# Convolution and low-rank mixer on one core: PSUM as one ring of four buffers, second product lagging by half a group, convolution a round earlier

## The chip, the cores and the metric

The kernel runs on one core of a Trainium2 chip. The metric is the device time of the kernel in microseconds. Before the change it is 365.75 us, the median of three runs (364.59, 365.75, 366.5). A trace of one further execution shows when each engine worked: TensorE (PE, with its weight loads as PEld), VectorE (DVE), ScalarE (ACT), GpSimd (POOL) and SyncE (SP, which only issues DMAs here).

## The reference

The input x has 8 batches of 4224 rows and 192 columns. It goes through a causal depthwise convolution of 7 taps, with softmaxed weights shared by the 24 columns of each of 8 heads, and then through a mixer: a low-rank product along the rows (rank 32), an add, and a two-layer product along the columns with a relu between.

```
w = softmax(weight)                       # 8 heads x 7 taps
y[b,s,h,:] = sum_k w[h,k] * xpad[b,s+k,h,:]
h = (y^T @ U @ V)^T                       # U: 4224 x 32, V: 32 x 4224
u = y + h
out = u + relu(u @ w_ch1) @ w_ch2         # 192 -> 768 -> 192
```

## The kernel before

The rows of all batches are cut into 264 tiles of 128 rows, 33 per batch, and 8 tiles make a group: 33 groups. The instructions of each engine run in the order in which the program writes them (manual_schedule), and a loop of 34 rounds (L596 to L613) writes that order out. Round g does the following:

- `mix_quad(g + 2)` (L414), twice, ahead of the chunks and behind them: four matmuls for the low-rank product of four tiles (L426), and two VectorE adds of y into u (L438, or three with L446 where a batch ends between two tiles).
- `h1_chunk(g, m)` for m = 0 to 5 (L486): six matmuls for the first product (L495), in three pairs that each work on the two halves of 64 rows at once, then a relu into rl_sb, on ScalarE for chunks 0, 2, 4 and 5 (L505) and on VectorE for chunks 1 and 3 (L507).
- `w2_step(g - 1, n)` for n = 0 to 47, six in each of eight pieces (L509): the second product of the group one round back. Six matmuls make one tile (L516). After every second tile VectorE adds u and writes o_sb (L525), and SP stores it (L532).
- between the pieces, steps for other batches, sorted by piece: `turn_by_dma(g + 2)` after piece 2 (a transposing DMA on SP, L477), and, for the next batch nb, the convolution and the low-rank product.

A convolution unit `conv_two` (L326) makes two heads of 21 or 12 tiles with two matmuls of 504 or 288 columns (L336) and one eviction to y (ScalarE L346; VectorE L348 only for batches 0 and 1). A batch has eight units. Rows at the start of each tile, which need the tile before, come from `conv_halo` (L352): eight matmuls (L359), two ScalarE copies (L368) and a store on SP to a scratch in memory (L376). `put_halo` (L379) writes them over y with a DMA on SP (L380), after all units. `low_rank` (L385, matmuls L393) then reduces y over the batch, and `fold` (L405) finishes it. With last = 33*nb//8 - 3, that is 1, 5, 9, 13, 17, 21 and 25 for batches 1 to 7, the units of batch nb run in rounds last-4 to last-1, two in each, put_halo after piece 5 of round last-1, low_rank after piece 3 and fold after piece 5 of round last. Batch 1 has all units in round 0; batch 0 is made before the loop.

x is loaded by POOL's queue (L85) into two buffers, so the load of batch nb+2 waits for the convolution of batch nb; the rows for the halo go through a scratch in memory, with a load on POOL (L94) and a second on SP (L99). These loads are written at the end of round last of batch nb. y has three buffers, u five, uT four, rl_sb two, o_sb six.

PSUM has eight banks. Six are three buffers of two banks each (`big`, L71), used by everything but the second product, taken in turn. The other two are two buffers of one bank (`chps`, L514), each for two tiles of the second product. An allocation waits until the engines are done with the one whose buffer it takes.

Of the kernel before, what the change touches and what calls it, by code (L numbers as in the profile page):

```python
# [11 lines left out]
F32 = mybir.dt.float32  # L12
# [3 lines left out]
def kernel(  # L16
# [11 lines left out]
    P = nc.NUM_PARTITIONS  # L28

    B, S, D = x.shape  # L30
# [5 lines left out]
    HB = P // 2  # L36
# [6 lines left out]
    NG = NTOT // GT  # L43
# [21 lines left out]
    rls = ctx.enter_context(tc.tile_pool(name="rls", bufs=2))  # L65
    outs = ctx.enter_context(tc.tile_pool(name="outs", bufs=6))

    big_ps = ctx.enter_context(tc.tile_pool(name="big_ps", bufs=3, space=bass.MemoryType.PSUM))
    w2_ps = ctx.enter_context(tc.tile_pool(name="w2_ps", bufs=2, space=bass.MemoryType.PSUM))

    def big(dtype=F32):  # L71
        return big_ps.tile([P, 2, BK * 4 // mybir.dt.size(dtype)], dtype, name="big")
# [8 lines left out]
    def new_x(b):  # L81
        x_tiles[b] = xs.tile([P, NT + 1, D], BF16, name="x_sb")

    def load_x(b, s0, s1):
        nc.gpsimd.dma_start(  # L85
            out=x_tiles[b][:, 1 + s0 : 1 + s1, :],
            in_=x[b, s0 * P : s1 * P, :].rearrange("(j p) d -> p j d", p=P),
        )

    def load_halo(b):  # L90

        hx_dr = dram.tile([HP, NT - 1, D], BF16, name="hx_dr")
        src = x[b, P - HALO : P - HALO + HP, :]
        nc.gpsimd.dma_start(  # L94
            out=hx_dr[:],
            in_=bass.AP(src.tensor, src.offset, [[D, HP], [P * D, NT - 1], [1, D]]),
        )
        hx = hxs.tile([HJ * HP, HS, D], BF16, name="hx_sb")
        nc.sync.dma_start(out=hx[:], in_=hx_dr[:].rearrange("p (j s) d -> (p j) s d", s=HS))  # L99
        hx_tiles[b] = hx  # L100
# [122 lines left out]
    for c in range(KC):  # L223
# [10 lines left out]
        in0=cps[:, 0, 0 : KC * H]  # L234
# [9 lines left out]
    for q in range(P // Q):  # L244
        rows = slice(q * Q, (q + 1) * Q)
        n = SP if q < P // Q - 1 else Q
# [79 lines left out]
    def conv_two(b, s0, s1, hh, on_act, bands):  # L326

        if b not in y_tiles:
            y_tiles[b] = ys.tile([P, NT, D], BF16, name="y_sb")
        x_sb, y_sb = x_tiles[b], y_tiles[b]  # L330
        n = (s1 - s0) * GS
        cps = big()
        for q in range(2):
            hc = slice((hh + q) * GS, (hh + q + 1) * GS)
            for w in range(bands):
                nc.tensor.matmul(  # L336
                    out=cps[:, q, 0:n],
                    lhsT=band_sb[:, hh + q, w, :],
                    rhs=x_sb[:, 1 + s0 - w : 1 + s1 - w, hc],
                    start=(w == 0),  # L340
                    stop=(w == bands - 1),
                )
        src = cps[:, :, 0:n].rearrange("p q (j c) -> p q j c", c=GS)
        dst = y_sb[:, s0:s1, hh * GS : (hh + 2) * GS].rearrange("p j (q c) -> p q j c", q=2)
        if on_act:
            nc.scalar.activation(out=dst, in_=src, func=ACT.Copy)  # L346
        else:
            nc.vector.tensor_copy(out=dst, in_=src)  # L348
# [3 lines left out]
    def conv_halo(b):  # L352

        hx = hx_tiles[b]
        n = HALO * HJ
        hps = big()
        H2 = H // 2
        for hh in range(H):
            nc.tensor.matmul(  # L359
                out=hps[:, hh // H2, (hh % H2) * HS * GS : (hh % H2 + 1) * HS * GS],  # L360
                lhsT=halo_band[:, hh, :],
                rhs=hx[:, :, hh * GS : (hh + 1) * GS],
                start=True,
                stop=True,
            )
        hy = hys.tile([n, HS, D], BF16, name="hy_sb")
        for h in range(2):
            nc.scalar.activation(  # L368
                out=hy[:, :, h * H2 * GS : (h + 1) * H2 * GS].rearrange(
                    "p s (h c) -> p h s c", c=GS  # L370
                ),
                in_=hps[0:n, h, 0 : H2 * HS * GS].rearrange("p (h s c) -> p h s c", s=HS, c=GS),
                func=ACT.Copy,
            )
        hy_dr = dram.tile([n, HS, D], BF16, name="hy_dr")
        nc.sync.dma_start(out=hy_dr[:], in_=hy[:])  # L376
        hy_tiles[b] = hy_dr

    def put_halo(b):  # L379
        nc.sync.dma_start(  # L380
            out=y_tiles[b][0:HALO, 1:NT, :],
            in_=hy_tiles[b][:].rearrange("(c j) s d -> c (j s) d", j=HJ),
        )

    def low_rank(b, j0, j1):  # L385
        y_sb = y_tiles[b]
        n = P // R
        if b not in tps_tiles:
            tps_tiles[b] = big()
        tps = tps_tiles[b]  # L390
        for j in range(j0, j1):
            q = j % n
            nc.tensor.matmul(  # L393
                out=tps[q * R : (q + 1) * R, 0, 0:D],
                lhsT=U_by_tile[:, :, j],
                rhs=y_sb[:, j, :],
                start=(j < n),
                stop=(j >= NT - n),
            )
        if j1 == NT:  # L400
            tf = tfs.tile([P, D], F32, name="tf_sb")
            nc.vector.tensor_copy(out=tf[:], in_=tps[:, 0, 0:D])  # L402
            tt_tiles[b] = tf
# [80 lines left out]
    rl_tiles, ch_tiles = {}, {}  # L484
# [24 lines left out]
    def w2_step(g, n):  # L509

        t, m = divmod(n, MC)
        i = t // 2
        if t % 2 == 0 and m == 0:
            ch_tiles[g, i] = w2_ps.tile([P, 2, D], F32, name="chps")  # L514
        chps = ch_tiles[g, i]
        nc.tensor.matmul(  # L516
            out=chps[:, t % 2, :],
            lhsT=rl_tiles[g][:, m, t, :],
            rhs=W2_sb[:, m, :],
            start=(m == 0),  # L520
            stop=(m == MC - 1),
        )
        if t % 2 == 1 and m == MC - 1:
            o_sb = outs.tile([P, 2, D], F32, name="o_sb")
            nc.vector.tensor_tensor(  # L525
                out=o_sb[:].rearrange("p t (k r) -> p t k r", r=HB),
                in0=chps[:].rearrange("p t (k r) -> p t k r", r=HB),
                in1=u_tiles[g][:, i].rearrange("p k t r -> p t k r"),
                op=ALU.add,
            )  # L530
            r0 = (g * GT + 2 * i) * P
            nc.sync.dma_start(  # L532
                out=out_rows[r0 : r0 + 2 * P, :].rearrange("(s p) d -> p s d", p=P),
                in_=o_sb[:],
            )
# [3 lines left out]
    i = 0  # L539
# [15 lines left out]
    load_halo(2)  # L555


    W2N = GT * MC
    PIECE = MC
    NP = W2N // PIECE  # L560
    END = 1000
# [3 lines left out]
    def add(g, piece, step):  # L565
        beside[g].append((piece, step))
# [3 lines left out]
        add(g, 2, lambda g=g: turn_by_dma(g + AHEAD))  # L570
    for nb in range(1, B):
        last = (nb * NT) // GT - AHEAD - 1
        rounds = [0] if nb == 1 else list(range(last - 4, last))
        if nb == 1:
            add(rounds[0], 1, build_halo_band)
        add(rounds[0], 1, lambda nb=nb: conv_halo(nb))
        for n, g in enumerate(rounds):
            share = units[len(units) * n // len(rounds) : len(units) * (n + 1) // len(rounds)]
            for e, u in enumerate(share):
                on_act = nb > 1 or e % 2 == 1  # L580
                add(g, 2 + 2 * e, lambda nb=nb, u=u, a=on_act: conv_two(nb, *u, a, 1))
        add(rounds[-1], 5 if nb > 1 else END, lambda nb=nb: put_halo(nb))
        if nb + 2 < B:
            add(
                last,
                END,
                lambda nb=nb: (
                    new_x(nb + 2),
                    [load_x(nb + 2, *s) for s in blocks],
                    load_halo(nb + 2),  # L590
                ),
            )
        add(last, 3, lambda nb=nb: low_rank(nb, 0, NT))
        add(last, 5, lambda nb=nb: fold(nb))

    for g in range(NG + 1):  # L596
        if g < NG:
            ahead = g + AHEAD < NG
            if ahead:
                mix_quad(g + AHEAD, 0)  # L600
            for m in range(MC):
                h1_chunk(g, m)
            if ahead:
                mix_quad(g + AHEAD, QT)
        steps = sorted(beside[g], key=lambda s: s[0])
        for i in range(NP):
            if g > 0:
                for n in range(i * PIECE, (i + 1) * PIECE):
                    w2_step(g - 1, n)
            while steps and steps[0][0] <= i:  # L610
                steps.pop(0)[1]()
        for _, step in steps:
            step()  # L613
# [30 lines left out]
```

## Time and profile before

| what | value |
|---|---|
| median of three runs | 365.75 us |
| profiled execution | 365.63 us, span 363.9 us |
| TensorE clock granted, mean | 0.981 |
| second product, L516 | 1584 matmuls, 247 ns each by the trace |
| first product, L495 | 1188 matmuls, 380 ns each |
| relu on ScalarE, L505 / VectorE, L507 | 1022 ns x132 / 1225 ns x66 |
| add and output, L525 | 558 ns x132 |
| add into u, L438 | 549 ns x128 |
| eviction of a unit, L346 | 1011 ns (504 columns a head), 651 ns (288) |

The span runs from the first to the last instruction; the profiled execution's own time is 1.7 us longer. Matmuls overlap one another, so their durations add up to more than the time between them; the times between starts tell how fast TensorE goes. DMA issues and waits of a queue do not count as busy. A line of the timeline reads: start, length, engine, line, operation, what is written from what, shapes, count, and in brackets the idle time of the engine before it with what ended it. A line of the stretches reads: stretch, length, then for PE, PEld, DVE, ACT and POOL the busy time and the number of instructions, the granted clock, the DMA engines' share and GB/s.

### The profile page before, as it was taken

To read this page: it belongs to the slowest core of one execution; us is meant where nothing else is said; L and a number is where in the kernel's file an instruction comes from. 1 tells how busy PE (TensorE), PEld (TensorE's weight loads), DVE (VectorE), ACT (ScalarE), POOL (GpSimd) and SP (SyncE) were. 2 spreads that over 40 slices of the span, in tenths; PEclk is the share of its full clock that TensorE was granted. 3 is DMA by queue.
4 is the path that set the end of the run, shared out by engine and by line. 5 is a ranking of instruction groups with operands and counts; after the bars stand their busy time and mean duration, and the time that the engine had idled before them with its cause. 6 is when DMAs were issued, how large, how long until landed. Compare 5 with 4: busy or idle time off the path is not lost.

```text
span 363.9 us, 8526 instructions
## 1 busy us (share of the span) xinstructions
PE 340.9 (94%) x3601; PEld 234.1 (64%) x3601; DVE 237.5 (65%) x382; ACT 195.2 (54%) x213; POOL 33.7 (9%) x55
## 2 busy tenths in 40 slices
PE   2849799999999999997999999999999999999995
PEld 2524476666667676774667676676666666777775
DVE  4426766777667756775567756776767767777553
ACT  7504866656565555556365556556565534444440
POOL 7830210003000300021000300000000000000000
PEclk9986999999999999999899999999999999999999
DMA  7999999659986799859977599754455665556525
GB/s 96 188 213 198 140 161 191 173 128 192 197 212 131 125 213 166 200 94 194 186 129 195 99 219 202 140 137 132 107 131 130 141 131 131 130 131 132 131 88 174
DMA packets 125066, 56.51 MB, mean 155 GB/s; under 512 B 89832, under 2 KB 124824, under 8 KB 124888
## 3 DMA queue, kind: packets, MB, share of 16 engines
q1 hardware_dynamic: 86100, 40.81, 49.4%
q0 software_dynamic: 38864, 15.14, 35.4%
q8 instruction: 28, 0.46, 0.6%
q14 instruction: 11, 0.09, 0.1%
q10 hardware_dynamic: 63, 0.00, 0.0%
HBM read 31.85 MB, written 27.50 MB: 163 GB/s over the span
## 4 chain that ended last, share of the span: by engine, by line
PE 83%; DMA 9%; DVE 3%; POOL 1%; ACT 1%; issue 1%; SPq 0%; POOLq 0%; DVEq 0%
PE chps L516 36%; PE big L495 34%; PE big L336 5%; DMA y_sb<-hy_dr 4%; PE big L426 4%; DMA x_sb<-in_x_dram 3%; DMA V_sb<-V_sb 2%; PE big L393 2%; PE big L407 1%; DVE o_sb L525 1%; DVE rl_sb L507 1%; POOL x_sb L85 1%; DVE y_sb L348 1%; ACT rl_sb L505 1%; PE big L461 1%
## 5 line engine op out<-in xcount | busy, mean ns | idle before, releaser
L505 ACT ACTIVATE rl_sb<-big 128x1024 bf16<-128x1024 f32 x132 | 131.5, 1022 | 100.1 <-PE big L495 71.1
L516 PE MATMUL chps<-W_sb,rl_sb 128*128 128x192 bf16 x1584 | 148.4, 247 | 0.0
L495 PE MATMUL big<-uT_sb,W_sb 64*128 64x512 bf16 x1188 | 143.6, 380 | 0.9 <-DVE y_sb L348 0.3
L516 PEld LDWEIGHTS <-rl_sb 128*128 128x128 bf16 x1584 | 131.1, 98 | 14.0 <-issue 6.3
L525 DVE TENSOR_TENSOR o_sb<-chps,u_sb 128x384 f32<-128x384 f32 x132 | 73.6, 558 | 70.5 <-PE chps L516 68.3
L495 PEld LDWEIGHTS <-W_sb 64*128 64x128 bf16 x1188 | 61.6, 95 | 69.6 <-DVE u_sb L438 14.4
L507 DVE TENSOR_SCALAR rl_sb<-big 128x1024 bf16<-128x1024 f32 x66 | 80.8, 1225 | 14.5 <-PE big L495 14.2
L438 DVE TENSOR_TENSOR u_sb<-y_sb,big 128x384 bf16<-128x384 bf16 x128 | 64.8, 549 | 17.7 <-PE big L426 17.7
L346 ACT ACTIVATE y_sb<-big 128x576 bf16<-128x576 f32 (+3 forms) x58 | 46.8, 808 | 43.6 <-PE big L336 43.2
L336 PE MATMUL big<-x_sb,band_sb 128*128 128x288 bf16 (+3 forms) x160 | 35.6, 331 | 2.6 <-ACT halo_band L212 1.1
L85 POOL DMA_DIRECT2D x_sb<-in_x_dram x17 | 20.4, 1201 | 171.8 <-PE big L336 149.0
L426 PE MATMUL big<-tt_sb,V_sb 64*128 64x192 bf16 x264 | 23.1, 253 | 5.1 <-DMA V_sb<-V_sb 3.9
L426 PEld LDWEIGHTS <-V_sb 64*128 64x128 bf16 x264 | 11.0, 96 | 21.5 <-issue 13.6
L336 PEld LDWEIGHTS <-band_sb 128*128 128x128 bf16 x160 | 15.2, 102 | 6.9 <-issue 1.7
L348 DVE CAST y_sb<-big 128x576 bf16<-128x576 f32 (+3 forms) x10 | 8.0, 816 | 6.3 <-PE big L336 6.2
L393 PE MATMUL big<-y_sb,U_sb 128*32 128x192 bf16 x264 | 9.1, 261 | 2.2 <-DMA y_sb<-hy_dr 2.2
L393 PEld LDWEIGHTS <-U_sb 128*32 128x32 bf16 x264 | 7.1, 169 | 4.0 <-issue 3.8
L368 ACT ACTIVATE hy_sb<-big 48x384 bf16<-48x384 f32 x14 | 6.0, 478 | 2.7 <-PE big L359 2.7
L402 DVE COPY tf_sb<-big 128x192 f32<-128x192 f32 x8 | 2.9, 358 | 6.7 <-PE big L393 6.7
L224 PE MATMUL big<-taps,at_tap 7*128 7x8 bf16 x7 | 0.3, 162 | 6.6 <-DVE taps L207 6.6
L470 ACT ACTIVATE uT_sb<-big 128x768 bf16<-128x768 bf16 x1 | 0.8, 811 | 9.9 <-DVE uT_sb L469 9.9
L407 PE MATMUL big<-tf_sb,fold_sb 128*128 128x192 f32 x16 | 4.6, 370 | 0.5 <-DVE tf_sb L402 0.5
(57 smaller groups left out, 54.5 us busy)
## 6 DMA issues: line engine op xcount, KB each, us to landing
out_dram<-o_sb SPq DMA_DIRECT2D x132, 192.0 KB, 2.6
x_sb<-in_x_dram POOLq DMA_DIRECT2D x7, 1008.0 KB, 12.8
x_sb<-in_x_dram POOLq DMA_DIRECT2D x8, 576.0 KB, 17.3
hx_dr<-in_x_dram POOLq DMA_DIRECT2D x7, 144.0 KB, 18.1
hx_sb<-hx_dr SPq DMA_DIRECT2D x7, 144.0 KB, 3.4
x_sb<-in_x_dram POOLq DMA_DIRECT2D x1, 624.0 KB, 8.1
W_sb<-in_moe_w_ch_dram POOLq DMA_DIRECT2D x2, 288.0 KB, 13.8
hy_dr<-hy_sb SPq DMA_DIRECT2D x7, 72.0 KB, 5.7
```

The source lines that it names most:

```text
L85: nc.gpsimd.dma_start(out=x_tiles[b][:, 1 + s0 : 1 + s1, :], in_=x[b, s0 * P : s1 * P, :].rearrange("(j p) d -> p j d", p=P),)
L336: nc.tensor.matmul(out=cps[:, q, 0:n], lhsT=band_sb[:, hh + q, w, :], rhs=x_sb[:, 1 + s0 - w : 1 + s1 - w, hc], start=(w == 0), stop=(w == ...
L346: nc.scalar.activation(out=dst, in_=src, func=ACT.Copy)
L348: nc.vector.tensor_copy(out=dst, in_=src)
L393: nc.tensor.matmul(out=tps[q * R : (q + 1) * R, 0, 0:D], lhsT=U_by_tile[:, :, j], rhs=y_sb[:, j, :], start=(j < n), stop=(j >= NT - n),)
L426: nc.tensor.matmul(out=ups[:, t, i * D : (i + 1) * D], lhsT=V_sb[rows, j * P : (j + 1) * P], rhs=tt_tiles[b][rows, :], start=True, stop=True,)
L438: nc.vector.tensor_tensor(out=dst, in0=y_tiles[b][:, j : j + 2, :].rearrange("p t (k r) -> p t k r", r=HB), in1=add, op=ALU.add,)
L495: nc.tensor.matmul(out=h1[:, q, :], lhsT=W1_sb[rows, k, m * P : (m + 1) * P], rhs=ut[rows, :, k, :], start=(k == 0), stop=(k == KB - 1),)
L505: nc.scalar.activation(out=rl, in_=src, func=ACT.Relu)
L507: nc.vector.tensor_scalar_max(out=rl, in0=src, scalar1=0.0)
L516: nc.tensor.matmul(out=chps[:, t % 2, :], lhsT=rl_tiles[g][:, m, t, :], rhs=W2_sb[:, m, :], start=(m == 0), stop=(m == MC - 1),)
L525: nc.vector.tensor_tensor(out=o_sb[:].rearrange("p t (k r) -> p t k r", r=HB), in0=chps[:].rearrange("p t (k r) -> p t k r", r=HB), in1=u_ ...
```

## The change

The pool for `chps` is gone and `big` has four buffers of two banks. The second product of a group takes two such buffers, one for each half (four tiles, two in each bank).

The second product now runs in two halves. Pieces 0 to 3 of round g do steps 24 to 47 of group g-1; pieces 4 to 7 do steps 0 to 23 of group g, whose first product was made in the same round. Round 0, which had none of it, does the first half of group 0, and the last round does only the second half of group 32.

The units of batch nb (from 2 on) run in rounds last-5 to last-2, and for batch 2, where there is no round 0 left for them, in rounds 1 to 3, with two, three and three units. conv_halo goes with the first of these rounds, put_halo after piece 6 of the last of them. low_rank, fold and the place where the loads are written stay where they were.

```diff
-    big_ps = ctx.enter_context(tc.tile_pool(name="big_ps", bufs=3, space=bass.MemoryType.PSUM))
-    w2_ps = ctx.enter_context(tc.tile_pool(name="w2_ps", bufs=2, space=bass.MemoryType.PSUM))
+    big_ps = ctx.enter_context(tc.tile_pool(name="big_ps", bufs=4, space=bass.MemoryType.PSUM))
...
         t, m = divmod(n, MC)
         i = t // 2
-        if t % 2 == 0 and m == 0:
-            ch_tiles[g, i] = w2_ps.tile([P, 2, D], F32, name="chps")
-        chps = ch_tiles[g, i]
+        if t % 4 == 0 and m == 0:
+            ch_tiles[g, t // 4] = big()
+        chps = ch_tiles[g, t // 4][:, i % 2, 0 : 2 * D].rearrange("p (t d) -> p t d", d=D)
...
-                in0=chps[:].rearrange("p t (k r) -> p t k r", r=HB),
+                in0=chps.rearrange("p t (k r) -> p t k r", r=HB),
...
-        rounds = [0] if nb == 1 else list(range(last - 4, last))
+        rounds = [0] if nb == 1 else list(range(max(1, last - 5), last - 1))
...
-        add(rounds[-1], 5 if nb > 1 else END, lambda nb=nb: put_halo(nb))
+        add(rounds[-1], 6 if nb > 1 else END, lambda nb=nb: put_halo(nb))
...
         for i in range(NP):
-            if g > 0:
-                for n in range(i * PIECE, (i + 1) * PIECE):
-                    w2_step(g - 1, n)
+            gg, n0 = (g - 1, W2N // 2) if i < NP // 2 else (g, -W2N // 2)
+            if 0 <= gg < NG:
+                for n in range(n0 + i * PIECE, n0 + (i + 1) * PIECE):
+                    w2_step(gg, n)
             while steps and steps[0][0] <= i:
                 steps.pop(0)[1]()
```

## The prediction

> **What bounds the kernel now.** I read the share of each engine on the page first, then the chain, then the round lengths by stretches of time, then one round of the timeline, and last who waits on TensorE.
>
> ```profile
> PE 340.9 (94%) x3601; PEld 234.1 (64%) x3601; DVE 237.5 (65%) x382; ACT 195.2 (54%) x213; POOL 33.7 (9%) x55
> ...
> PE 83%; DMA 9%; DVE 3%; POOL 1%; ACT 1%; issue 1%; SPq 0%; POOLq 0%; DVEq 0%
> ```
>
> TensorE is the bound: nearly the whole chain is its work. Whether anything is left inside these 94% must be seen from starts, because matmul ends overlap. Three rounds in stretches: one without convolution, then the rounds of the low rank product for batches 4 and 6.
>
> ```profile
> 304.57:313.34 8.77, 8.76 (x97) 6.06 (x94) 6.62 (x11) 3.99 (x4) 0.00 (x0) 1.00 0.55 136
> ...
> 162.84:178.12 15.28, 13.25 (x143) 9.10 (x141) 7.34 (x13) 6.87 (x8) 2.02 (x3) 0.89 1.32 188
> 246.00:257.42 11.42, 11.41 (x144) 7.91 (x141) 7.26 (x13) 6.87 (x8) 0.00 (x0) 1.00 0.58 147
> ```
>
> The columns are length, busy PE, PEld, DVE, ACT, POOL, clock, DMA. The two low rank rounds do the same work; one is 3.86 us longer and its clock is 0.89. Now the steady round, which begins at 313.16:
>
> ```profile
> 313.16 0.34 PE L426 MATMUL big<-tt_sb,V_sb 64*128 64x192 bf16 x4
> ...
> 313.27 0.56 DVE L525 TENSOR_TENSOR o_sb<-chps,u_sb 128x384 f32<-128x384 f32 x1 [0.43 <-PE chps L516]
> 313.34 4.32 PE L495 MATMUL big<-uT_sb,W_sb 64*128 64x512 bf16 x36
> 313.74 1.01 DVE L438 TENSOR_TENSOR u_sb<-y_sb,big 128x384 bf16<-128x384 bf16 x2
> ...
> 314.81 1.19 PEld L495 LDWEIGHTS <-W_sb 64*128 64x128 bf16 x13 [0.50 <-DVE u_sb L438]
> 314.91 1.23 DVE L507 TENSOR_SCALAR rl_sb<-big 128x1024 bf16<-128x1024 f32 x1 [0.16 <-PE big L495]
> ...
> 316.19 0.97 PEld L495 LDWEIGHTS <-W_sb 64*128 64x128 bf16 x11 [0.20 <-issue]
> 316.32 1.23 DVE L507 TENSOR_SCALAR rl_sb<-big 128x1024 bf16<-128x1024 f32 x1 [0.18 <-PE big L495]
> ...
> 317.60 0.34 PE L426 MATMUL big<-tt_sb,V_sb 64*128 64x192 bf16 x4
> ```
>
> Narrow stretches of the timeline put the pairs of L495 at 313.34, 313.56, 313.77: 0.215 us each, three pairs a chunk, so six chunks need 3.87 us, but mix_quad follows 317.60-313.34 = 4.26 us after the first. Three stops make the difference, each 0.05 us after VectorE frees the buffer of three allocations ago: chunk 2 at 314.81 behind mix_quad's adds (ended 314.75), 0.18 late; chunk 4 at 316.19 behind the relu of chunk 1 (316.14), 0.08 late; mix_quad at 317.60 behind the relu of chunk 3 (317.55), 0.11 late. Together 0.37 us a round. And TensorE's waits name one DMA:
>
> ```profile
> PE big L393 <- DMA y_sb<-hy_dr: 2.2, 2, 2.0
> ```
>
> **The change part by part.** The profiled execution took 365.63 us (span 363.9), 0.12 under the median of 365.75, so the sum against it serves for both.
>
> *Ring of four.* Instructions stay the same. A round now allocates mix_quad, six chunks, mix_quad, and two halves of the second product; each waits for the one four before. I set the start of the last second-product matmul at 0: its add runs 0.28 to 0.84, mix_quad's adds to 1.76, the relu of chunk 1 from 1.92 to 3.15, that of chunk 3 to 4.4. Chunk 3 starts at 2.29 and needs the adds of 1.76; chunk 5 at 3.58 needs 3.20; the second mix_quad at 4.22 needs ScalarE's relu of chunk 2, 3.6; the first half of the second product at 4.48 needs 4.42 (chunk 3, with the 0.05). All fit, the last by 0.06. So the 0.37 goes, less 0.01 for that thin margin: 0.36 x 29 (rounds 2 to 30) = -10.4 us. What is late next is nothing in the round but the change of matmul kind (0.17 instead of 0.09 at 317.87), which stays. Bounds: nothing gained if the two new tenants use up the fourth buffer (0), all gained (-10.7). I take -10.4, since each wait was worked out. Rounds 31 and 32 have one such stop each of 0.2 (-0.4), round 1 one of 0.15.
>
> *New tenants.* A half's buffer is held until its second add, 0.89 us after the last matmul's start, by the same rows. In the rounds with convolution of the halo (batches 3 to 7) the second unit comes four allocations behind the first half and only 0.58 us after it: 0.31 x 5 = +1.5. In rounds 2 and 3, with three units, chunk 0 comes four behind the second half and would start at 0.35: 0.54 x 2 = +1.1. With two units chunk 1 (1.0) needs 0.89: fits. Bounds: 0 if buffers are taken in the order in which they were freed, and twice if VectorE is late; I take +2.6.
>
> *Half a group of lag.* 24 of the second product's matmuls (0.083 each, 4.07/48; 2.0 us) leave the end and go into round 0, beside convolutions that wait for evictions there (TensorE stops 0.3 to 0.4 us four times between 39.5 and 42.5). The tail runs with TensorE alone, so -2.0 there. In round 0 I follow the order: the transposes and the halo band begin 0.4 earlier with the fourth buffer, the 2.0 us go in, the two adds (1.1 us) lengthen VectorE's queue, and round 1's chunk 0 starts at 44.6 instead of 43.72: +0.9. The relu of chunk 5 ends 1.4 us after mix_quad starts (318.99 against 317.60), and the first matmul of the new half that reads it would come 2.6 us after: the 24 matmuls of the older half cover it. Without them it would come 0.7 us after, and cost 0.7 a round. Out DMAs on SP keep their rhythm of four a round. Bounds: 0 to -2.0, taken -1.1.
>
> *Convolution a round earlier.* The DMA wait goes: the halo rows are put at the end of round last-2, and their 7 to 8 us (issue 83.69, use 91.03) get a whole round (9.3) more. Worth 3.86 for batch 4 by the rows above, and 0.38, 0.10 and 0.15 for batches 2, 3 and 5, by their rounds against 11.42: -4.5. The 3.86 is more than the idle 2.0 because the clock drops behind it:
>
> ```profile
> 170.52:172.54 2.02, 0.01 (x3) 0.00 (x1) 0.37 (x1) 0.33 (x1) 0.00 (x0) 1.00 1.40 224
> 172.54:176.50 3.96, 3.96 (x49) 3.10 (x49) 0.88 (x2) 1.01 (x1) 0.00 (x0) 0.67 1.39 210
> ```
>
> The Trainium skill, "TensorE: Matmul & The Clock Gate" (Part 1), has the clock halve after an idle window of about 3.4 us; here 2.0 us was enough, so the measurement decides. By the page the clock would be another matter that stays, and the sum 1.6 us higher.
>
> What else moves: 8 matmuls, two ScalarE evictions and SP's store of the halo product, all before the second unit in a round that had the same pieces; ScalarE has 3.99 of 8.77 us busy, so they cost TensorE time only, as before. POOL's loads of batch 4 and later wait for the buffer of the batch two before, and so start a round earlier with it: their lead on the convolution stays. Batch 3's does not move (43.7); SP passes its halo on at 62.84 and round 4 needs it near 78. SP's load of the halo keeps its place at the end of round last, where it has waited 51.1 us in 7 times with stores queued behind it; for batches 4 to 7 its data now comes a round sooner, which TensorE doesn't see, with four stores a round and six output buffers. Put_halo on SP now stands behind one more second-product add; that is hidden by the extra round, and costs at most the 3.86 if that cover is gone.
>
> Sum: -10.4 -0.55 +2.6 -1.1 -4.5 = -13.95; 365.63 - 13.95 = 351.7 us.
>
> **Rivals.**
> *Hand-over by the buffer (slower).* The two halves of a buffer now have a writer and a reader at once: VectorE adds from its first bank while TensorE should write the second. If the wait is kept for the whole buffer, each half group stops after its second tile from 0.08 to 0.89: 0.81 x 66 = 53, giving 405 us. It decides from 0.21 us a stop on. For it: no row of before shows such a pair in PSUM. Against it: L426 on partitions 0 to 63 of V_sb ran at 21.1 while the copy to 64 to 127 landed only at 25.2, so waits go by parts of a tile. The Trainium skill, "PSUM — Partial Sum Buffer" (PSUM bank collisions raise a hardware error), wants such guards by bank, which this layout meets; by that rule the stop is nought.
>
> *The ring gives nothing back.* The buffers that hold sums are missing elsewhere: 365.63 -4.5 -1.1 = 360.0. For it: a half is held over 2.8 us. Against it: every releaser in the shown round precedes its need.
>
> *VectorE becomes the bound.* 6.62 of 8.41 us is 79%, and its queue is in order. Where margins of 0.06 and 0.1 break by 0.2 a round: 29 x 0.2 = 5.8, so 357.5.
>
> *The halo wait stays,* because the DMA is issued late on SP all the same: 351.7 + 4.5 = 356.2. Against it: SP's queue has a round more.
>
> **How the numbers follow.** Forecast 0.64, no gain by the ring 0.15, VectorE 0.08, halo 0.03, hand-over 0.08, something slower elsewhere 0.02. The forecast's own range is 349 (no new waits) to 357. From 348 to 361 it holds all but the slower cases and a little. A difference under 0.5% (1.8 us) can't be told from none: 0.03 of the cases near 360 and beyond are given to it. Faster 0.87, same 0.03, slower 0.10.
>
> **What would show it.** Rounds without convolution of 8.4 us instead of 8.77; no idle of the weight loads behind L438 inside L495; low rank rounds near 11.05 without a DMA wait and with the clock at 1.00; a tail of 24 instead of 48 matmuls behind the last round's. Wrong it would be with idle TensorE between the second and third tile of a half, or with chunks waiting for the adds of L525.

## The result, and the profile after

The changed kernel takes 400.27 us in the median (396.46 to 402.58) against 365.91 us before (now four runs): a ratio of 1.091, 95% interval 1.081 to 1.101. It is slower by 34 us where 14 us less were forecast. The profiled execution took 402.12 us. Ratios here and below are of fast runs alone, which leaves out one of these four (402.58 us), while medians and ranges are of all runs.

The changed kernel's page, engine shares and the chain that ended last:

```profile
PE 337.7 (84%) x3601; PEld 230.9 (58%) x3601; DVE 237.2 (59%) x382; ACT 194.8 (49%) x213; POOL 33.8 (8%) x55
...
PE 78%; DVE 11%; DMA 7%; issue 2%; POOL 1%; ACT 1%; SPq 0%; POOLq 0%; DVEq 0%
```

The instructions are the same in number, and no engine does more work; but TensorE now stands still for 63 us of the span instead of 23, and VectorE has 11% of the chain instead of 3%. Stretches of the changed kernel (columns as before: length, PE, PEld, DVE, ACT, POOL, clock, DMA): round 1, the low rank round of batch 4, and a round without convolution.

```profile
45.15:62.87 17.72, 13.16 (x145) 9.19 (x142) 7.14 (x13) 7.25 (x9) 3.14 (x3) 0.90 1.30 176
...
183.06:194.96 11.90, 10.96 (x135) 7.40 (x133) 7.25 (x13) 6.01 (x6) 0.00 (x0) 1.00 1.14 195
...
334.62:344.62 10.00, 8.70 (x96) 5.96 (x94) 6.62 (x11) 3.99 (x4) 0.00 (x0) 1.00 0.48 120
```

The round without convolution takes 10.00 us; it was 8.77 and was to be 8.4. Batch 4's low rank round no longer has the long DMA wait. Round 1 takes 17.72 us; in the kernel before it was this:

```profile
43.72:54.94 11.22, 11.20 (x140) 7.99 (x141) 6.71 (x12) 6.96 (x9) 3.09 (x3) 1.00 1.28 166
```

TensorE's part of the timeline for one round of the changed kernel, where all lines are one less than before (L515 is the second product, L524 its add):

```profile
344.62 4.05 PE L494 MATMUL big<-uT_sb,W_sb 64*128 64x512 bf16 x36
348.51 0.33 PE L425 MATMUL big<-tt_sb,V_sb 64*128 64x192 bf16 x4
348.77 1.16 PE L515 MATMUL big<-W_sb,rl_sb 128*128 128x192 bf16 x12
350.58 2.14 PE L515 MATMUL big<-W_sb,rl_sb 128*128 128x192 bf16 x24 [0.65 <-DVE o_sb L524]
353.37 1.15 PE L515 MATMUL big<-W_sb,rl_sb 128*128 128x192 bf16 x12 [0.65 <-DVE o_sb L524]
354.45 0.34 PE L425 MATMUL big<-tt_sb,V_sb 64*128 64x192 bf16 x4
```

The first product now runs in 3.89 us from its first start to mix_quad's (it was 4.26): the three stops that the ring was to remove are gone. But the second product stops twice, each time after 12 matmuls, two tiles, which is just where a half group passes from the first bank of its buffer to the second. It waits for the add that reads the first bank. Between starts, such a stop is 0.894 us instead of 0.083, so 0.81 us. TensorE's waits over the whole run count them:

```profile
PE big L515 <- DVE o_sb L524: 38.2, 66, 0.7
...
PE big L392 <- DMA y_sb<-hy_dr: 4.0, 1, 4.0
```

66 is two for each of 33 groups. (The view counts from the modelled end of a matmul, hence 0.65 instead of 0.81.) By starts, 53 of them stand free at 0.81 us, and 13 are covered in part by the halo product or the fold, which lie between the two tiles there (0.46 us left in each): 43.0 + 6.0 = 49.0 us. The wait of 4.0 us for the halo rows is in round 1; there was none there before.

### The profile page after: what moved, and what is told of

Its sections match the earlier page's. It is cut to its first block, busy times and chain, and to the rows that moved or that the text cites. A ratio compares the mean times of both kernels' runs of the same rounds, so it can differ in the third digit from the quotient of the medians.

```text
span 400.4 us, 8501 instructions
## 1 busy us (share of the span) xinstructions
PE 337.7 (84%) x3601; PEld 230.9 (58%) x3601; DVE 237.2 (59%) x382; ACT 194.8 (49%) x213; POOL 33.8 (8%) x55
## 3 DMA queue, kind: packets, MB, share of 16 engines
q1 hardware_dynamic: 86100, 40.81, 44.5%
## 4 chain that ended last, share of the span: by engine, by line
PE 78%; DVE 11%; DMA 7%; issue 2%; POOL 1%; ACT 1%; SPq 0%; POOLq 0%; DVEq 0%
PE big L515 36%; PE big L494 32%; DVE o_sb L524 9%; PE big L335 5%; PE big L425 3%; DMA x_sb<-in_x_dram 3%; DMA y_sb<-hy_dr 2%; DMA V_sb<-V_sb 2%; PE big L392 2%; PE big L460 1%; POOL x_sb L84 1%; ACT y_sb L345 0%; POOL in_band L153 0%; DVE rl_sb L506 0%; DVE u_sb L437 0%
## 5 line engine op out<-in xcount | busy, mean ns | idle before, releaser
L515 PE MATMUL big<-W_sb,rl_sb 128*128 128x192 bf16 x1584 | 157.4, 247 | 38.2 <-DVE o_sb L524 38.2
L515 PEld LDWEIGHTS <-rl_sb 128*128 128x128 bf16 x1584 | 131.9, 98 | 62.7 <-issue 54.7
L524 DVE TENSOR_TENSOR o_sb<-big,u_sb 128x384 f32<-128x384 f32 x132 | 73.7, 558 | 117.2 <-PE big L515 113.5
L494 PE MATMUL big<-uT_sb,W_sb 64*128 64x512 bf16 x1188 | 134.9, 379 | 0.4 <-ACT uT_sb L469 0.4
L494 PEld LDWEIGHTS <-W_sb 64*128 64x128 bf16 x1188 | 58.2, 95 | 63.9 <-issue 2.2
L93 POOL DMA_DIRECT2D hx_dr<-in_x_dram x7 | 4.9, 700 | 0.0
```

Source lines behind the costliest of these rows:

```text
L494: nc.tensor.matmul(out=h1[:, q, :], lhsT=W1_sb[rows, k, m * P : (m + 1) * P], rhs=ut[rows, :, k, :], start=(k == 0), stop=(k == KB - 1),)
L515: nc.tensor.matmul(out=chps[:, t % 2, :], lhsT=rl_tiles[g][:, m, t, :], rhs=W2_sb[:, m, :], start=(m == 0), stop=(m == MC - 1),)
L524: nc.vector.tensor_tensor(out=o_sb[:].rearrange("p t (k r) -> p t k r", r=HB), in0=chps.rearrange("p t (k r) -> p t k r", r=HB), in1=u_til ...
```

## The experiments

Theory A: the loss is the hand-over inside one buffer, TensorE writing one bank of it while VectorE has still to read the other. Rival B: a ring that carries the sums is itself the loss, since it leaves too few buffers for the rest. Rival C: the lag or the moved convolution is the loss. Each run's ratio is to runs of the kernel before that were taken along with it.

**A buffer of its own for each pair of tiles** (in the changed kernel):

```diff
-        if t % 4 == 0 and m == 0:
-            ch_tiles[g, t // 4] = big()
-        chps = ch_tiles[g, t // 4][:, i % 2, 0 : 2 * D].rearrange("p (t d) -> p t d", d=D)
+        if t % 2 == 0 and m == 0:
+            ch_tiles[g, i] = big()
+        chps = ch_tiles[g, i][:, 0, 0 : 2 * D].rearrange("p (t d) -> p t d", d=D)
```

> The changed kernel, but each pair of tiles of the second product takes a buffer of its own from the ring of four, so that no matmul writes into a buffer that an add has still to read. Theory A (the hand-over inside one buffer is the loss: the third tile's first matmul waits 0.81 us for the add of the first two): the stops go, rounds without convolution fall from 10.0 to about 8.4 us, and the time to 355 us (349 by the forecast without new tenants' waits, and some 6 for the halo of batch 1, which comes late on SP and stops TensorE 4.2 us at 52.6). Rival B (a ring that carries the sums is itself the loss): the time stays at 395 to 402 us. Rival C (the half-group lag or the moved convolution is the loss): also 395 to 402.

Measured: 353.18 us (352.03 to 354.29), ratio to before 0.966 (0.959 to 0.973). Four tenants of the ring per round instead of two, so by rival B it should have been no better. The run's stretches (round 1, a round without convolution) and one round of its timeline:

```profile
44.31:59.74 15.43, 12.83 (x143) 9.10 (x141) 7.14 (x13) 7.26 (x9) 3.14 (x3) 0.89 1.33 178
...
303.40:311.79 8.39, 8.39 (x96) 5.94 (x94) 6.63 (x11) 3.99 (x4) 0.00 (x0) 1.00 0.57 143
```

```profile
303.40 4.05 PE L494 MATMUL big<-uT_sb,W_sb 64*128 64x512 bf16 x36
307.29 0.33 PE L425 MATMUL big<-tt_sb,V_sb 64*128 64x192 bf16 x4
307.55 4.13 PE L515 MATMUL big<-W_sb,rl_sb 128*128 128x192 bf16 x48
```

All 48 matmuls run in one piece. The round is 8.39 us against 10.00: the difference of 1.61 is two stops of 0.81. Theory A holds and B falls.

**Same shared buffers, both adds after the half's last matmul** (in the changed kernel):

```diff
-        if t % 2 == 1 and m == MC - 1:
-            o_sb = outs.tile([P, 2, D], F32, name="o_sb")
+        if t % 4 == 3 and m == MC - 1:
+            for i in (i - 1, i):
+                chps = ch_tiles[g, t // 4][:, i % 2, 0 : 2 * D].rearrange("p (t d) -> p t d", d=D)
+                o_sb = outs.tile([P, 2, D], F32, name="o_sb")
...
```

(the add and the store follow inside the loop, as they were)

> The changed kernel, with the same shared buffers, but both adds of a half come after its last matmul, so that nothing is written behind a read. Theory A: the 66 stops go too, but a buffer is held until two adds behind its last matmul (1.36 us after that matmul's start instead of 0.89), which chunk 1 of the next round meets 0.36 us too early in the rounds with two units, and the second unit by 0.8 us in five rounds: 362 to 368 us, above the run with a buffer for each pair. Rival B or C: 395 to 402 us.

Measured: 354.82 us (353.01 to 359.15), ratio 0.968 (0.960 to 0.976). With the write no longer behind a read, the shared buffer costs next to nothing. The expectation's extra 9 to 15 us for the longer hold did not come: rounds with two units took 8.91 us, against 8.88 to 8.92 in the run above. So the buffer that chunk 1 takes is probably not that of the half which my rule of "the one four before" named; the traces do not show which buffer an allocation gets.

**The ring alone** (in the kernel before; the first two hunks of the change and the add's operand):

```diff
-    big_ps = ctx.enter_context(tc.tile_pool(name="big_ps", bufs=3, space=bass.MemoryType.PSUM))
-    w2_ps = ctx.enter_context(tc.tile_pool(name="w2_ps", bufs=2, space=bass.MemoryType.PSUM))
+    big_ps = ctx.enter_context(tc.tile_pool(name="big_ps", bufs=4, space=bass.MemoryType.PSUM))
...
+        if t % 4 == 0 and m == 0:
+            ch_tiles[g, t // 4] = big()
```

> The kernel before, with only the ring of four two-bank buffers (a half group of the second product in one buffer); lag of a whole group and the old place of the convolution. Theory A: 366 less 10 for the free chunks, and 52 hand-overs of 0.81 us that nothing covers (66 less those with the halo product or the fold between the two tiles): 366 - 10 + 42 = 398 us (393 to 405), with rounds without convolution of 10.0 us. Rival C (lag or convolution is the loss): 350 to 360 us.

Measured: 405.27 us (402.73 to 405.76), ratio 1.106 (1.099 to 1.114). The ring with shared halves alone makes the whole loss, and rounds without convolution take 10.00 us: rival C falls too. It is 7 us over the estimate, which had no term for the second of these waits:

```profile
PE big L515 <- DVE o_sb L524: 38.0, 65, 0.7
PE big L392 <- DMA y_sb<-hy_dr: 8.7, 1, 8.7
```

The wait for batch 1's halo rows, 0 in the kernel before and 4.0 in the changed one, is 8.7 here, though this run moves no step of the convolution. The product that needs them begins at 48.3 us, 2.6 us sooner than in the kernel before (50.9), since round 0 is shorter. But the larger part is that the put leaves SP at 49.6, 5.1 us later than there (44.5): the transposing DMA ahead of it holds SP for 4.7 us instead of 1.6, and then SP waits 1.6 us for the store of the halo product to land. Why these two were slower here is not known.

**The convolution alone, a round earlier** (in the kernel before, the two hunks `rounds = ...` and `add(rounds[-1], 6 ...)` of the change):

> The kernel before, with only the convolution of batches 2 to 7 a round earlier. By the forecast's term: the DMA waits of batches 2 to 5 go, 4.5 us less by the profile: 361.4 us (359 to 363), low rank rounds of 11.4 us. If the wait for batch 4 was of that one execution alone, 364 to 366; rival C: above 370.

Measured: 362.05 us (361.11 to 365.35), ratio 0.991 (0.987 to 0.995), that is 3.3 us less, with 1.9 to 4.7 in the interval. Low rank rounds take 11.0 to 11.2 us, less than the 11.4 expected, since the eight matmuls of the next batch's halo product are now a round earlier; the halo wait is 0.4 us in all.

**The half-group lag alone** (in the kernel before, the last hunk of the change):

> The kernel before, with only the half-group lag; PSUM and the convolution as before, so there is no hand-over inside a buffer. By the forecast's term: 24 matmuls less behind the last round (2.0 us), 0.9 us more in round 0: 1 us less than before. Against it the two stores that now stand ahead of the halo rows of batch 1 on SP and their DMA's 7 to 8 us: a stop of 1 to 5 us in round 1, with a slower clock behind it. 364 to 370 us. If the lag itself were a loss (rival C): above 385.

Measured: 362.32 us (361.15 to 363.81), ratio 0.990 (0.988 to 0.993). From the first product of the last group to the end of the span it takes 14.14 us instead of 16.09, the 2.0 us that were forecast. But round 0 takes 15.77 us instead of 13.62, so the lag itself is not where the run's gain comes from. Most of the gain is in batch 4's round, 11.81 us where the profile of before had 15.28; the halo waits are 0.4 us in all, where it had 2.2. That is not one lucky execution, since all ten runs lie below all thirteen of the kernel before (363.97 and up), but why the halo rows are in time here is not shown. The stop that was expected in round 1 did not come: it took 11.20 us.

**One buffer of two banks in place of two of one bank** (in the kernel before; same banks, same order):

```diff
-    w2_ps = ctx.enter_context(tc.tile_pool(name="w2_ps", bufs=2, space=bass.MemoryType.PSUM))
+    w2_ps = ctx.enter_context(tc.tile_pool(name="w2_ps", bufs=1, space=bass.MemoryType.PSUM))
...
+    chall = w2_ps.tile([P, 2, BK], F32, name="chall")
...
-        chps = ch_tiles[g, i]
+        chps = chall[:, i % 2, 0 : 2 * D].rearrange("p (t d) -> p t d", d=D)
```

> The kernel before, in which the two one-bank buffers of the second product are made one buffer of two banks, taken once for the whole run: same banks, same order of all instructions, same lag. Theory A1 (a write into one bank waits for a read of the other when both lie in one buffer): a stop of 0.81 us at each change of bank, four in a round, the one between rounds hidden behind the first product: some 90 of them free of cover, so 366 + 73 = 439 us (425 to 450). Theory A2 (waits go by bank, and the stop of the changed kernel has another reason, such as the size of the buffer or its place in the ring): 364 to 370 us.

Measured: 433.52 us (433.42 and 433.62), ratio 1.186 (1.177 to 1.195). One round of its timeline:

```profile
347.89 1.16 PE L515 MATMUL chall<-W_sb,rl_sb 128*128 128x192 bf16 x12
349.70 1.15 PE L515 MATMUL chall<-W_sb,rl_sb 128*128 128x192 bf16 x12 [0.65 <-DVE o_sb L524]
351.50 1.15 PE L515 MATMUL chall<-W_sb,rl_sb 128*128 128x192 bf16 x12 [0.65 <-DVE o_sb L524]
353.30 1.15 PE L515 MATMUL chall<-W_sb,rl_sb 128*128 128x192 bf16 x12 [0.65 <-DVE o_sb L524]
```

In the kernel before, the 48 matmuls of a round ran in one piece:

```profile
317.87 4.13 PE L516 MATMUL chps<-W_sb,rl_sb 128*128 128x192 bf16 x48
```

This separates the buffer from the bank. The banks alternate as in the kernel before, which had no stop; only the boundary of the buffer is drawn otherwise, and there is a stop of 0.65 (0.81 by starts) at every change of bank. So the wait follows the buffer. It is a wait that the program carries between the add and the next write to the same buffer. This use of the two banks does not need it: in the kernel before VectorE's add ran from 319.07 us for 0.56 us, in the midst of the 48 matmuls, reading one bank while TensorE wrote the other.

**Batch 1's halo rows: the order on SP** (on the run with a buffer for each pair):

```diff
     def load_halo(b):
...
+        hx_drs[b] = hx_dr
+        if b != 2:
+            pass_halo(b)
+    def pass_halo(b):
         hx = hxs.tile([HJ * HP, HS, D], BF16, name="hx_sb")
-        nc.sync.dma_start(out=hx[:], in_=hx_dr[:].rearrange("p (j s) d -> (p j) s d", s=HS))
+        nc.sync.dma_start(out=hx[:], in_=hx_drs[b][:].rearrange("p (j s) d -> (p j) s d", s=HS))
...
         add(rounds[0], 1, lambda nb=nb: conv_halo(nb))
+        if nb == 1:
+            add(rounds[0], 2, lambda: pass_halo(2))
```

> The run with a buffer for each pair, and SP's load of the halo rows of batch 2 moved behind the store of the halo product of batch 1, after piece 2 of round 0. Theory: SP stands in its queue from 31 to 42.5 us for batch 2's rows, and the store of batch 1's halo product, whose data is there at 39.8, stands behind it. The store then goes out at 40, the put at 45.6 to 46.5, and the stop of 2.9 us in round 1 becomes 0 to 2 us, the slow clock behind it goes where the stop is short: 348 to 352 us, against 353.2. Rival: the put itself waits for the evictions of round 0 and its DMA takes 7.7 us, so nothing changes: 353.

Measured: 347.64 us (345.40 to 348.11), ratio 0.950 (0.944 to 0.955). SP's queue in the changed kernel, then in this run (L375 and L382 are the store of batch 1's halo product, L98 and L105 the load of batch 2's rows, L379 and L386 the put):

```profile
44.45 0.31 SPq L98 DMA_DIRECT2D hx_sb<-hx_dr  x1
44.80 0.43 SPq L375 DMA_DIRECT2D hy_dr<-hy_sb  x1
45.27 1.58 SPq L476 DMA_TRANSPOSE uT_sb<-u_sb  x1
46.96 1.82 SPq L531 DMA_DIRECT2D out_dram<-o_sb  x2
48.95 0.34 SPq L379 DMA_DIRECT2D y_sb<-hy_dr  x1
```

```profile
39.19 0.31 SPq L382 DMA_DIRECT2D hy_dr<-hy_sb  x1
39.54 2.26 SPq L483 DMA_TRANSPOSE uT_sb<-u_sb  x1
42.77 0.31 SPq L105 DMA_DIRECT2D hx_sb<-hx_dr  x1
43.20 0.92 SPq L538 DMA_DIRECT2D out_dram<-o_sb  x2
44.30 0.34 SPq L386 DMA_DIRECT2D y_sb<-hy_dr  x1
```

In the changed kernel the store stands until 44.8 behind a load whose rows have not come; here it leaves at 39.2 and the put at 44.3. (In the run with pair buffers, from which this one differs in the order alone, they left at 42.8 and 46.5, and TensorE waited 2.6 us.) TensorE no longer waits for the halo rows, and round 1 takes 11.06 us at full clock instead of 15.43:

```profile
43.75:54.81 11.06, 11.06 (x144) 8.11 (x142) 7.14 (x13) 7.27 (x9) 3.14 (x3) 1.00 1.22 175
```

This is the fastest version of all, 5% under the kernel before. One stop is new in its profile: round 6 takes 9.79 us, 8.92 in the run with pair buffers; there VectorE waits 1.9 us for a store to free an output buffer, and a chunk of the first product then waits 0.4 us for that add.

**The low rank product of batch 1 three pieces later, on top of that:**

```diff
-        add(last, 3, lambda nb=nb: low_rank(nb, 0, NT))
-        add(last, 5, lambda nb=nb: fold(nb))
+        add(last, 3 if nb > 1 else 6, lambda nb=nb: low_rank(nb, 0, NT))
+        add(last, 5 if nb > 1 else 7, lambda nb=nb: fold(nb))
```

> The same, and the low rank product of batch 1 moved from piece 3 to piece 6 of round 1, its fold from piece 5 to 7: 1.5 us of the second product and a convolution unit more ahead of it. The stop in round 1 should be gone (0 to 0.3 us) and the clock stay at 1.00: 347 to 350 us. If the stop is as long as before, the halo rows are late by more than their DMA.

Measured: 347.97 us (347.57 to 349.77), ratio 0.953 (0.947 to 0.959): no gain over the run above. Its profile has a stop of 1.1 us at that product (1.4 between starts); the expectation that it would be gone was wrong. Round 1 began 1.5 us sooner than in the run above (42.2 against 43.8), so the product came at 51.1, only 0.4 us later than there in spite of the three pieces. The put left at 44.9, 0.5 us later, and its rows were there at 52.5: 7.7 us behind the put, where the run above had them after at most 6.5 (44.3 to 50.8). Why the DMA took longer is not known.

**The ring alone, with a buffer for each pair** (in the kernel before: the first hunk of the change, and the allocation of the first experiment):

> The kernel before, with only the ring of four, each pair of tiles of the second product in a buffer of its own; lag and convolution as before. By the forecast's term the three stops of 0.37 us in a round go: rounds without convolution of 8.4 instead of 8.77 us, 10.4 us over the run. Against it, nothing moves the halo rows earlier here, so their DMA, which has its length whatever TensorE does, is met sooner: 9 us in round 1 (as in the run with the ring alone), and 0.5 to 3 us in the low rank rounds of batches 2 to 5, with the slow clock behind the longer ones. 355 to 364 us; below 354 if the halo rows do not matter.

Measured: 361.57 us (359.38 to 363.71), ratio 0.988 (0.982 to 0.994). Rounds without convolution are at 8.39 us, so some 11 us are won there, but most of it goes to waits for halo rows:

```profile
PE big L392 <- DMA y_sb<-hy_dr: 11.7, 5, 8.1
```

Round 1 takes 22.8 us and batch 4's low rank round 15.0. In round 1 the product begins at 48.6 us, 2.4 us sooner than in the kernel before, and the put leaves at 48.0, 3.5 us later.

## Why the prediction was wrong

The step that failed is in *Ring of four*: "each waits for the one four before", and from this "All fit". It looked for waits between the tenants of the ring and for none inside one, so that the sum has no term for the stop. The tile that the change makes of two banks has a reader and a writer in turn, and that hand-over costs 49.0 us. The forecast had it as its first rival, at 0.81 us a stop, 53 us and 405 us in all; the place, the price (0.81 measured) and the sign were right, and the chance of 0.08 was far too low. Two things had pushed it down. The row of V_sb shows waits by parts of a tile, but for a DMA's copy and a matmul on a tile in SBUF, not for TensorE and VectorE in PSUM. And the rule of the Trainium skill, "PSUM — Partial Sum Buffer", section on bank collisions, tells what the chip needs, a guard by bank; from it I took what the program does. The one-buffer run shows that the program waits by buffer; the rule itself is not touched by that, and the kernel before, which writes and reads two banks at once without a stop, agrees with it.

With that wait away, the terms can be read one by one:

- *Ring of four*, -10.4: right. 8.77 became 8.39 in rounds without convolution, 0.38 a round instead of 0.36; over 29 rounds 11.0 us. All three stops left together.
- *New tenants*, +2.6: nothing of it came. Rounds with two units take 10.50 us in the changed kernel, the 8.88 of the run with pair buffers and two stops of 0.81; rounds 2 and 3, where 0.54 each was expected, take 11.10 and 10.74 against 9.48 and 9.12, again just 1.62 more. The lower bound, 0, was the value. That buffers are taken in the order in which they were freed would explain it; that is argued, not shown.
- *Half a group of lag*, -1.1: the 2.0 us at the end came (1.95). Round 0 grew by 0.5 us in the changed kernel (14.16 against 13.62), where 0.9 was expected; but its first part, up to the second mix_quad, happened to run at a granted clock of 0.75 instead of 0.68 and was 0.8 us shorter (5.16 against 5.98). Behind that, at a clock of 1.00, it grew by 1.4 (9.00 against 7.64), and with the lag alone by 1.5 (9.10). So the term was about -0.5, inside its bounds.
- *Convolution a round earlier*, -4.5: the lone move gives -3.3, with -4.5 inside the interval. For batches 2 to 7 it did what was forecast. (Of the 3.86 us in batch 4's round, the clock's part is 1.8 us by the rows that the forecast shows, 3.86 less the idle 2.02, and not 1.6.)
- "Out DMAs on SP keep their rhythm of four a round": wrong for round 0, which had none of the second product's stores before and now has two, ahead of batch 1's put. The deeper cause is older: SP waits there for batch 2's rows, with batch 1's store behind it. In the kernel before, the put left at 44.5 us and the product came at 50.9, late enough. In the changed kernel the product comes 1.7 us later, at 52.6, but the put 4.5 us later, at 49.0: the load left SP 2.6 us later, and the two stores came in between. With the ring alone, where no store was added, the put was late too, and the product sooner. In the changed kernel round 1 takes 17.72 us against 11.06 where the order on SP is mended; 0.9 of that are two covered hand-overs, so some 5.8 us are this.

Put together, from the forecast: 351.7 + 49.0 (hand-overs) + 5.8 (batch 1) - 2.6 (tenants) - 0.6 (ring) = 403.3 us, against 402.12 of the profiled execution.

The sign was wrong, then, because of one wait that was seen, priced and thought unlikely. The mechanism that the forecast rested on is real: with a buffer for each pair it gives 353.2 us, 1.5 over the forecast, and 347.6 with SP's order mended. That 353.2 comes so near is in part luck: 2.6 us that did not come stand against 4.2 us of round 1 that the forecast did not have (15.43 against 11.22).

## What to carry to other kernels

When tiles that had buffers of their own are put into one larger buffer, ask who writes into it after somebody has begun to read it; if the program tracks such a buffer as a whole, the writer waits for the reader's full latency, here 0.81 us each time, and the cure is a buffer for each hand-over or all reads after all writes. A row that shows waits by parts for one memory and one pair of engines is no evidence for another pair. When a stage becomes faster, look for the DMA that it had been slow enough for, and for what stands ahead of that DMA in its queue: the ring with pair buffers alone kept 1.2% of some 3% because halo rows were met sooner and, in round 1, were sent later, and exchanging two DMAs in one queue gave 1.6% more.

## What the runs showed of the hardware

The granted clock of TensorE fell to half after pauses of about 2 us. Pauses of 0.4 us (ring with pair buffers alone, batch 2) and 1.1 us (later low rank product) left it at 1.00 in the stretch behind them; pauses of 1.9 us (adds last) and 2.6 us (pair buffers) gave 0.69 on average over the next 5.5 us, as the 2.0 us in the kernel before gave 0.67 over 3.96 us. In slices of half a microsecond it reads 0.50 there, from 174.04 to 177.04 us in the kernel before. The fall comes late: at about 173.9 us, 3.4 us after the pause began and 1.4 us after TensorE had gone on; in the other two 3.1 us after its beginning. The page of the Trainium skill "TensorE: Matmul & The Clock Gate" (Part 1) has the clock halve after an idle window of about 3.4 us; the pauses here were shorter, so the measurement decides. The stretches of the run with the later product and of that with the adds last, pause and what follows:

```profile
51.10:52.60 1.50, 0.40 (x7) 0.20 (x9) 0.21 (x1) 0.17 (x1) 0.00 (x0) 1.00 1.52 194
52.60:55.10 2.50, 2.22 (x44) 1.64 (x45) 1.18 (x3) 0.00 (x0) 0.00 (x0) 1.00 1.52 199
```

```profile
50.93:53.10 2.17, 0.29 (x3) 0.13 (x2) 1.02 (x2) 0.62 (x1) 0.00 (x0) 1.00 1.59 191
53.10:58.69 5.59, 5.59 (x64) 4.53 (x65) 0.79 (x3) 1.01 (x1) 0.00 (x0) 0.69 1.67 176
```

So a stop of 2.0 us cost nearly twice its length (3.86 us in batch 4's round before), and one of 0.81 us only itself (two made 1.61 us of a round). The 66 stops of the changed kernel left the clock at 1.00.
